# Seven half-size products for one more pair of row blocks, with the diagonal sums of two stages interleaved

## The chip, the cores and the metric

The kernel runs on one core of a Trainium2 chip. The metric is device time in microseconds (us) of one launch. Engines are named as in the profile: PE (TensorE matmuls), PEld (its weight loads), DVE (VectorE), ACT (ScalarE), POOL (GpSimd, which here also issues all large input loads) and SP (SyncE, which issues the output stores and the DMA transposes). The five engines run their own instruction streams in order and wait for one another through semaphores.

## The reference

A linear attention with decay (4 batches, 8 heads, 768 steps, head size 48) feeds a two-layer network with a leaky ReLU (384 to 2048 to 384, 3072 rows).

```python
# attention, for every batch and head
for t in range(768):
    cur = outer(u * k[t], v[t])
    y[t] = r[t] @ (state + cur)
    state = w[:, None] * state + outer(k[t], v[t])
# y is put side by side over the heads: x is 3072 x 384
h = x @ w_in                    # 384 x 2048
g = maximum(0.01 * h, h)
out = g @ w_out                 # 2048 x 384
```

## The kernel before

The 3072 rows are 24 **stages** of 128 steps (6 per batch) and 12 **pairs** of stages; pair m holds stages 2m and 2m+1. All compute is in bf16 with sums in fp32 in PSUM, which has eight banks, handed out in rotation by `next_bank`.

Work of a stage n, with the letter of its step:

- `prep` (P), DVE: r and k times powers of the decay, into `qk`; from stage 8 on, SP then turns it with a DMA transpose into `tp` (earlier stages use PE and ACT).
- `a_mm` (A), PE: the 128 x 128 scores of the eight heads, into two banks.
- `a_mask` (M), DVE: the scores are masked into `at`. From stage 8 on (`DIAG`), one predicated copy (line 408) writes the masked part over a tile that already holds the diagonal.
- `prep2` (Q): for stages below 8 it makes `vs`. From stage 8 on it makes the diagonal: three DVE operations, `ku = k*u` (line 346), `rku = r*ku` (348), and `s_tok`, the sum of `rku` over each head (350). Each needs the one before it, and a semaphore stands between them. Then `diag_tile` lays the eight sums on the diagonals of `at`: for stages 8 to 13 (below `LED`) POOL does it in two instructions (line 360), from 14 on ACT does it in eight (line 366).
- `kv_mm` (K), PE, and `state` (S), DVE: the new state from one bank and the old state (line 482, or lines 485 and 487).
- `y_part` (Y), PE and then ACT: the attention output, into `xT`.

Work of a pair: `g1_pair`, eight groups of six matmuls with `w_in` (line 562), each emptied by ACT with the leaky ReLU into `gT` (568); then the product with `w_out`, in one of two ways. `g2` (line 579) makes a stage's rows with 16 matmuls of 384 columns. `g2_seven` (line 643) makes a pair's four half-size blocks (128 rows x 192 columns each, 1024 of the 2048 inner terms at a time) out of seven products of 8 matmuls of 192 columns, in place of eight such products; for it DVE makes four sums of `gT` per pair (`g_sum`, line 617) and adds partial results from copies that ACT made (`keep`, line 651; `plus`, line 674). Its right-hand factors are four sums of `w_out`, made once by DVE (`w_sum`, line 599, four instructions). Before, pairs 4 to 11 use it (`SEVEN`).

The first stages are ordered by hand in `ORDER`, up to stage 9's masks. Then a loop over m from 3 to 11 emits, for one iteration: the eight `g1_pair` of pair m; the diagonal sums of stages 2m+4 and 2m+5 if they are below 14; the four `g_sum` of pair m-1 if it uses seven products; the diagonal sums of stages 2m+6 and 2m+7 if they are 14 or later; the loads of stages 2m+8 and 2m+9 (POOL, paced by the first group of pair m); scores and masks of stages 2m+4 and 2m+5; `y_part` of stages 2m+2 and 2m+3; `kv_mm` and `state` of 2m+4 and 2m+5; `prep` of 2m+6 and 2m+7; and last the product of pair m-1 with `w_out` (`second`). So pair 3's product is in the iteration of m = 4, between pairs 4 and 5 of `g1_pair`.

With seven products, one of the two `prep` and one of the two `state` are emitted inside `g2_seven`, and the 16 ACT tiles of stages 2m+6 and 2m+7 stand between its `keep` copies. `g2_seven` takes three banks: the two from which `y_part` was emptied, and the one from which the first `state` of the iteration reads. Its fourth product, `product(2, ...)`, writes that third bank:

```python
            product(1, 0, 0, True, False)
            keep(1, 1)
            some(3, 4)
            product(0, 1, 1, False, False)
            keep(0, 2)
            some(4, 16)
            product(2, (0, 1), (low, one), True, True)
            plus(2, 0, 0, 0)
```

Of the kernel before, what the change touches and what calls it, by code (L numbers as in the profile page):

```python
# [5 lines left out]
ALU = mybir.AluOpType  # L6
AF = mybir.ActivationFunctionType
AX = mybir.AxisListType
# [17 lines left out]
ORDER = """  # L26
P0 C F1 T0 P1 F1 T1.0 A0 T1.1 X0 M0 K0 W F1 V A1 Q0 X1 S0 Y0 M1 G0.0 K1 P2 T2 Q1 P3 Y1 T3 S1 X2 A2 M2 K2 G1.0 X3 A3 U J0.2 S2 Q2 M3 Y2 K3 P4
T4 Q3 J0.3 S3 Y3 J0.4 J0.5 J1.0 P5 A4 J1.1 P6 X4 M4 T5 X5 J1.2 K4 Q4 A5 S4 T6 J1.3 K5 J1.4 Y4 M5 L8 Q5 Y5 P7 J1.5 A6 J0.6 J2.0 J2.1 T7 M6 X6
X7 K6 J2.2 J2.3 A7 S6 J2.4 J2.5 L9 Q6 J0.7 J1.6 J2.6 M7 Z0 Z1 Z2 L10 J2.7 L11 J1.7 K7 S7 P8 Q7 Q8 P9 H0 Q9 K8 H1 P10 L12 K9 H2 S8 S9 Y6 Y7
A8 A9 P11 M8 H3 M9 L13  # L30
"""

# [5 lines left out]
class Sched:  # L38
# [8 lines left out]
    def add(self, eng, emit, R=(), W=(), dma=None):  # L47
        o = Op()
        o.eng, o.emit, o.dma, o.inc, o.val = eng, emit, dma, False, None
        deps = []  # L50
        for key in R:
            w = self.writer.get(key)
            if w is not None:
                deps.append((w, True))
        for key in W:
            w = self.writer.get(key)
            if w is not None:
                deps.append((w, False))
            for r in self.readers.get(key, ()):
                deps.append((r, False))  # L60
        o.deps = []
        for d, raw in deps:
            if d.dma is None and d.eng == eng and dma is None and (eng == "pe" or not raw):
                continue
            if d is not o and d not in o.deps:
                o.deps.append(d)
        for key in R:
            self.readers.setdefault(key, []).append(o)
        for key in W:
            self.writer[key] = o  # L70
            self.readers[key] = []
        self.ops.append(o)
        return o
# [47 lines left out]
def bass_rwkv5_eagle__then__act_leaky_relu_kernel(  # L121
# [13 lines left out]
    def SB(name, shape, dt=BF16):  # L135
        return ctx.enter_context(nc.sbuf_tensor(name, shape, dt))
# [1 line left out]
    NQK, NTP, NVS, NAT, NT, NX, NG, NO, NRK = 6, 6, 6, 6, 6, 3, 3, 4, 14  # L138
    TURNED, DIAG = 8, 8
    LED = 14  # L140
    SEVEN = (4, 5, 6, 7, 8, 9, 10, 11)
    HF, NH = NFB // 2, HD // 2
    w_in_sb = SB("w_in_sb", [128, NSL, DFF])
    w_out_sb = SB("w_out_sb", [128, NFB, HD])
# [24 lines left out]
    ident = SB("ident", [128, 128])  # L169
    ku = [SB(f"ku{i}", [128, HD]) for i in range(2)]  # L170
    rku = [SB(f"rku{i}", [128, HD]) for i in range(2)]
    s_tok = [SB(f"s_tok{i}", [128, H], FP32) for i in range(2)]
    qk = [SB(f"qk{i}", [128, 2 * H, E]) for i in range(NQK)]
    tp = [SB(f"tp{i}", [128, 2 * NP, 128]) for i in range(NTP)]
    vs = [SB(f"vs{i}", [128, HD]) for i in range(NVS)]
# [14 lines left out]
    add = sch.add  # L190
# [117 lines left out]
    def k_of(n):  # L308
        return k_sb[:, n % NRK, :] if n else k0_f[:, :]
# [26 lines left out]
    def prep2(n, whole=True):  # L336
        i2, iv = n % 2, n % NVS
        if n < DIAG:
            ps_s, key = kv_bank[n]
            s_of = ps_s[:, HD:HD + H]  # L340
            add("dve", lambda: V.tensor_tensor(hd(vs[iv][:, :]),  # L341
                                               v_sb[:, n, :].rearrange("p (h e) -> p h e", e=E)[:, :, 0:D],
                                               s_of.unsqueeze(2).to_broadcast([128, H, D]), ALU.mult),
                R=[("v", n), key], W=[("vs", iv)])
        else:
            add("dve", lambda: V.tensor_tensor(ku[i2][:, :], k_of(n), u_tab[:, :], ALU.mult),
                R=[("k", n % NRK), "u_tab"], W=[("ku", i2)])
            add("dve", lambda: V.tensor_tensor(rku[i2][:, :], r_of(n), ku[i2][:, :], ALU.mult),
                R=[("r", n % NRK), ("ku", i2)], W=[("rku", i2)])
            add("dve", lambda: V.tensor_reduce(s_tok[i2][:, :], hd(rku[i2][:, :]), AX.X, ALU.add),  # L350
                R=[("rku", i2)], W=[("s", i2)])
            if whole:
                diag_tile(n)

    def diag_tile(n, heads=range(H)):
        ia = n % NAT
        if n < LED:
            for hh in range(2):
                s_of = s_tok[n % 2][:, :].rearrange("p (m two) -> p two m", two=2)[:, hh, :]
                add("pool", lambda hh=hh, s_of=s_of: G.tensor_tensor(  # L360
                    at[ia][:, hh, :, :], ident[:, :].unsqueeze(1).to_broadcast([128, NP, 128]),
                    s_of.unsqueeze(2).to_broadcast([128, NP, 128]), ALU.mult),
                    R=["ident", ("s", n % 2)], W=[("at", ia, hh)])
            return
        for h in heads:
            add("act", lambda h=h: A.activation(at[ia][:, h % 2, h // 2, :], ident[:, :], AF.Copy,  # L366
                                                scale=s_tok[n % 2][:, h:h + 1]),
                R=["ident", ("s", n % 2)], W=[("at", ia, h % 2)])

    def turn(n, *halves):  # L370
        it, iq = n % NTP, n % NQK
# [363 lines left out]
    def u_table():  # L735
# [5 lines left out]
    steps = {"U": u_table, "V": u_cast, "P": prep, "Q": prep2, "T": turn, "A": a_mm, "M": a_mask, "K": kv_mm, "S": state, "Y": y_part, "X": diag, "C": decay_columns, "W": decay_table, "F": fill, "Z": w_sum,  # L741
             "G": g1, "J": g1_pair, "H": g2, "L": lambda n: load_stage(n, pace=[("pace", (n - 4) // 2, (n - 4) % 2)])}
    for name in ORDER.split():
        steps[name[0]](*(int(x) for x in name[1:].split(".") if x))
# [9 lines left out]
    for m in range(FIRST // 2, NST // 2):  # L754
        ahead = [n for n in (2 * m + 4, 2 * m + 5) if n < NST]
        further = [n for n in (2 * m + 6, 2 * m + 7) if LED <= n < NST]
        for j in range(8):
            g1_pair(m, j)
        for n in ahead:
            if n < LED:  # L760
                prep2(n)
        if m - 1 in SEVEN:
            for i in (0, 1, 3, 2):
                g_sum(m - 1, i)
        for n in further:
            prep2(n, False)
        for n in (2 * m + 8, 2 * m + 9):
            if n < NST:
                load_stage(n, pace=[("pace", 2 * m, 0)])
        for n in ahead:  # L770
            if n < DIAG:
                diag(n)
        for n in ahead:
            a_mm(n)
        for n in ahead:
            a_mask(n)
        y_first = taken[0] % 8
# [82 lines left out]
```

## Time and profile before

| | us |
|---|---|
| Median of 3 runs | 169.47 (167.68 to 171.02) |
| The profiled execution | 166.89 |
| Its span, first to last instruction | 165.0 |
| DVE busy in the span | 123.9 (75%) |
| ACT busy in the span | 116.3 (70%) |
| POOL busy in the span | 81.7 (50%) |

Times below are microseconds from the start of the span. In a row of the timeline stand start, busy time, engine, line and operation, and in brackets the engine's idle time before it and what ended it. In a row of the chain stand start, time, engine and line. An instruction's busy time can reach a little into the next one's, so the distance from start to start is what counts for an engine that has no pause.

### The profile page before, as it was taken

Reading aid. Unit: us, or ns where it says so; the run is one execution under the profiler, and the core shown is the slowest. Engines: PE = TensorE matmul, PEld = TensorE weight load, DVE = VectorE, ACT = ScalarE, POOL = GpSimd, SP = SyncE. Lnnn points to the kernel's source line nnn. Section 1 sums busy time; section 2 is a strip of 40 time slices with the busy share of each in tenths; the row PEclk is TensorE's granted clock in tenths of the full one; section 3 lists DMA queues with packets and bytes.
Section 4 is the critical chain, followed back from the end, with each engine's and each line's share of the span. In section 5 each row is a group of like instructions: output and inputs, shape, how many; then the busy total and the mean of one; then the engine's idle time right before and its main releaser. Section 6 shows DMA issues by size and latency. Waiting matters only on the chain.

```text
span 165.0 us, 5389 instructions
## 1 busy us (share of the span) xinstructions
PE 158.9 (96%) x2290; PEld 132.9 (81%) x2291; DVE 123.9 (75%) x238; ACT 116.3 (70%) x267; POOL 81.7 (50%) x97
## 2 busy tenths in 40 slices
PE   6979899999999999999999999999999999999993
PEld 3858678788666876876889889899899899898993
DVE  7797938657999979999668998878999467045253
ACT  4767588789113861989889989989999836828530
POOL 7999999992279989992750930920000000000000
PEclk9999999999999999999999999999999999999999
DMA  5999999999999999999995994996308102002022
GB/s 95 133 150 156 171 149 172 198 193 143 147 171 203 121 89 118 136 169 140 187 127 73 176 131 92 190 92 119 107 4 177 49 0 99 0 7 93 0 99 95
DMA packets 99260, 19.68 MB, mean 119 GB/s; under 512 B 92323, under 2 KB 99237, under 8 KB 99237
## 3 DMA queue, kind: packets, MB, share of 16 engines
q0 software_dynamic: 76512, 10.03, 96.9%
q1 hardware_dynamic: 21682, 9.11, 27.1%
q8 instruction: 18, 0.29, 0.8%
q10 hardware_dynamic: 1042, 0.20, 0.6%
q14 instruction: 6, 0.04, 0.1%
HBM read 20.45 MB, written 4.72 MB: 152 GB/s over the span
## 4 chain that ended last, share of the span: by engine, by line
PE 93%; DVE 4%; ACT 2%; issue 1%
PE ps_all L562 37%; PE ps_all L643 23%; PE ps_all L579 13%; PE ps_all L517 7%; PE ps_all L398 5%; PE ps_all L378 2%; PE ps_all L432 2%; DVE at L416 2%; PE ps_all L255 1%; ACT tp L385 1%; PE ps_all L295 1%; PE ps_all L456 1%; DVE vs L341 1%; PE ps_all L545 1%; ACT gT L568 0%
## 5 line engine op out<-in xcount | busy, mean ns | idle before, releaser
L562 PE MATMUL ps_all<-xT,w_in_sb 128*128 128x256 bf16 x564 | 64.8, 273 | 0.0
L562 PEld LDWEIGHTS ps_all<-xT,w_in_sb 128*128 128x128 bf16 x564 | 54.4, 98 | 7.1 <-DMA w_in_sb<-in_moe_w_in_dram 0.2
L568 ACT ACTIVATE gT<-ps_all 128x512 bf16<-128x512 f32 x94 | 54.7, 596 | 6.6 <-PE ps_all L562 3.0
L218 POOL DMA_DIRECT2D rk_sb<-in_k_dram x23 | 21.7, 942 | 17.0 <-PE ps_all L562 17.0
L366 ACT ACTIVATE at<-ident,s_tok 128x128 bf16<-128x128 bf16 x80 | 25.0, 390 | 0.0
L408 DVE CAST_PREDICATED at<-mask,ps_all 128x1024 bf16<-128x1024 uint16 x16 | 18.8, 1219 | 6.6 <-PE ps_all L398 6.5
L218 POOL DMA_DIRECT2D v_sb<-in_v_dram x24 | 22.7, 953 | 0.8 <-POOLq L845 0.8
L579 PE MATMUL ps_all<-w_out_sb,gT 128*128 128x384 bf16 x128 | 21.8, 326 | 0.0
L218 POOL DMA_DIRECT2D rk_sb<-in_r_dram x23 | 21.6, 943 | 0.0
L674 DVE TENSOR_TENSOR out_sb<-ps_all,snap 128x192 f32<-128x192 f32 x25 | 8.8, 356 | 14.9 <-PE ps_all L643 14.3
L579 PEld LDWEIGHTS ps_all<-w_out_sb,gT 128*128 128x128 bf16 x128 | 12.2, 98 | 7.7
L643 PE MATMUL ps_all<-tw,gs 128*128 128x192 bf16 x192 | 18.3, 246 | 0.0
L360 POOL TENSOR_TENSOR at<-ident,s_tok 128x512 bf16<-128x512 bf16 x12 | 13.4, 1142 | 8.2 <-DVE s_tok L350 8.2
L643 PEld LDWEIGHTS ps_all<-tw,gs 128*128 128x128 bf16 x192 | 16.1, 98 | 0.0
L585 ACT ACTIVATE out_sb<-ps_all 128x384 f32<-128x384 f32 x8 | 3.9, 488 | 14.6 <-PE ps_all L579 14.6
L532 ACT ACTIVATE xT<-ps_all 128x384 bf16<-128x384 f32 x24 | 11.0, 490 | 4.4 <-PE ps_all L517 4.1
L643 PE MATMUL ps_all<-w_out_sb,gT 128*128 128x192 bf16 x128 | 13.2, 246 | 0.0
L617 DVE TENSOR_TENSOR gs<-gT 128x1024 bf16<-128x1024 bf16 x16 | 10.9, 684 | 2.9 <-ACT gT L568 2.9
L517 PE MATMUL ps_all<-at,v_sb 128*32 128x128 bf16 x384 | 11.9, 224 | 0.3 <-DVE vs L341 0.2
L416 DVE TENSOR_TENSOR at<-ps_all,mask 128x512 bf16<-128x512 f32 x16 | 10.3, 682 | 2.1 <-PE ps_all L398 2.1
L651 ACT ACTIVATE snap<-ps_all 128x192 f32<-128x192 f32 x24 | 7.9, 330 | 4.8 <-PE ps_all L643 4.4
L517 PEld LDWEIGHTS ps_all<-at,v_sb 128*32 128x32 bf16 x384 | 9.1, 98 | 2.7 <-DVE vs L341 0.9
(80 smaller groups left out, 224.8 us busy)
## 6 DMA issues: line engine op xcount, KB each, us to landing
out_dram<-out_sb SPq DMA_DIRECT2D x22, 192.0 KB, 3.1
v_sb<-in_v_dram POOLq DMA_DIRECT2D x24, 96.0 KB, 5.5
rk_sb<-in_r_dram POOLq DMA_DIRECT2D x23, 96.0 KB, 5.8
rk_sb<-in_k_dram POOLq DMA_DIRECT2D x23, 96.0 KB, 5.6
w_in_sb<-in_moe_w_in_dram POOLq DMA_DIRECT2D x4, 384.0 KB, 6.6
w_out_sb<-in_moe_w_out_dram POOLq DMA_DIRECT2D x4, 384.0 KB, 10.3
out_dram<-out_sb SPq DMA_DIRECT2D x4, 96.0 KB, 1.6
tp<-qk SPq DMA_TRANSPOSE x16, 3.6
```

Source lines behind the costliest of these rows:

```text
L218: add("pool", lambda: G.dma_start(dst, src), R=pace, W=[key], dma=f"{which}{n}")
L360: add("pool", lambda hh=hh, s_of=s_of: G.tensor_tensor(at[ia][:, hh, :, :], ident[:, :].unsqueeze(1).to_broadcast([128, NP, 128]), s_of.un ...
L366: add("act", lambda h=h: A.activation(at[ia][:, h % 2, h // 2, :], ident[:, :], AF.Copy, scale=s_tok[n % 2][:, h:h + 1]), R=["ident", ("s" ...
L408: add("dve", lambda: V.copy_predicated(at[n % NAT][:, :, :, :].rearrange("p two m i -> p (two m) i"), mask[:, :].bitcast(mybir.dt.uint16). ...
L416: add("dve", lambda hh=hh, part=part: V.tensor_tensor(at[n % NAT][:, hh, :, :], part, mask[:, :].unsqueeze(1).to_broadcast([128, NP, 128]) ...
L517: last = PE.matmul(ps_y[32 * q:32 * q + 32, 128 * s:128 * s + 128], a, m, start=first_mm, stop=last_mm)
L532: add("act", lambda: A.activation(xT[m % NX][:, :, 128 * half:128 * half + 128], ps_y[:, 0:HD].rearrange("p (s t) -> p s t", t=128), AF.Copy),
L562: last = PE.matmul(ps_g[:, 256 * f:256 * f + 256], w_in_sb[:, s, 128 * fb:128 * fb + 128], xT[ix][:, s, :], start=s == 0, stop=s == NSL - 1)
L568: add("act", lambda: A.activation(gT[ig][:, 2 * j:2 * j + 2, :].rearrange("p f t -> p (f t)"), ps_g[:, :], AF.Prelu, alpha=0.01), R=[key], ...
L579: last = PE.matmul(ps_o[:, 0:HD], gT[ig][:, s, 128 * half:128 * half + 128], w_out_sb[:, s, :], start=s == 0, stop=s == NFB - 1)
L617: add("dve", lambda: V.tensor_tensor(x[i][:, :, :], a, b, op), R=keys, W=[("gs", m % 2, i)])
L643: done = PE.matmul(ps_o[:, 0:NH], lhs[:, s, :], rhs[:, s, :], start=first and s == 0, stop=s == HF - 1, skip_group_check=not (first and last))
```

## The change

Pair 3 joins the pairs with seven products. The three DVE operations of the diagonal sums are split into steps (`bonus`) and emitted for the two stages of a pair in alternation (`bonus_pair`), with the diagonal tiles of both stages behind them; `s_tok` gets four buffers in place of two. In `ORDER`, stage 9's `prep` goes ahead of the diagonal sums of stages 8 and 9, which are now together ahead of stage 4's product with `w_out`. The fourth `w_sum`, which ran behind the masks, states and `prep` of the iteration of m = 3, goes ahead of the masks of stages 10 and 11 in that iteration.

```diff
@@ ORDER
-X7 K6 J2.2 J2.3 A7 S6 J2.4 J2.5 L9 Q6 J0.7 J1.6 J2.6 M7 Z0 Z1 Z2 L10 J2.7 L11 J1.7 K7 S7 P8 Q7 Q8 P9 H0 Q9 K8 H1 P10 L12 K9 H2 S8 S9 Y6 Y7
+X7 K6 J2.2 J2.3 A7 S6 J2.4 J2.5 L9 Q6 J0.7 J1.6 J2.6 M7 Z0 Z1 Z2 L10 J2.7 L11 J1.7 K7 S7 P8 Q7 P9 B8 H0 K8 H1 P10 L12 K9 H2 S8 S9 Y6 Y7
...
-    SEVEN = (4, 5, 6, 7, 8, 9, 10, 11)
+    SEVEN = (3, 4, 5, 6, 7, 8, 9, 10, 11)
...
-    s_tok = [SB(f"s_tok{i}", [128, H], FP32) for i in range(2)]
+    s_tok = [SB(f"s_tok{i}", [128, H], FP32) for i in range(4)]
...
         else:
+            for step in range(3):
+                bonus(n, step)
+            if whole:
+                diag_tile(n)
+
+    def bonus(n, step):
+        i2, i4 = n % 2, n % 4
+        if step == 0:
             add("dve", lambda: V.tensor_tensor(ku[i2][:, :], k_of(n), u_tab[:, :], ALU.mult),
                 R=[("k", n % NRK), "u_tab"], W=[("ku", i2)])
+        elif step == 1:
             add("dve", lambda: V.tensor_tensor(rku[i2][:, :], r_of(n), ku[i2][:, :], ALU.mult),
                 R=[("r", n % NRK), ("ku", i2)], W=[("rku", i2)])
-            add("dve", lambda: V.tensor_reduce(s_tok[i2][:, :], hd(rku[i2][:, :]), AX.X, ALU.add),
-                R=[("rku", i2)], W=[("s", i2)])
-            if whole:
-                diag_tile(n)
+        else:
+            add("dve", lambda: V.tensor_reduce(s_tok[i4][:, :], hd(rku[i2][:, :]), AX.X, ALU.add),
+                R=[("rku", i2)], W=[("s", i4)])
+
+    def bonus_pair(n, whole=True):
+        for step in range(3):
+            bonus(n, step)
+            bonus(n + 1, step)
+        if whole:
+            diag_tile(n)
+            diag_tile(n + 1)
...
-        for n in ahead:
-            if n < LED:
-                prep2(n)
+        if ahead and ahead[0] < LED:
+            bonus_pair(ahead[0])
+        if m == 3:
+            w_sum(3)
         if m - 1 in SEVEN:
             for i in (0, 1, 3, 2):
                 g_sum(m - 1, i)
-        for n in further:
-            prep2(n, False)
+        if further:
+            bonus_pair(further[0], False)
...
         for n in coming[:at_once]:
             prep(n)
-        if m == 3:
-            w_sum(3)
```

More of the change, by code (lines that the diff above doesn't have):

```diff
@@ L358, in diag_tile @@
             for hh in range(2):
-                s_of = s_tok[n % 2][:, :].rearrange("p (m two) -> p two m", two=2)[:, hh, :]
+                s_of = s_tok[n % 4][:, :].rearrange("p (m two) -> p two m", two=2)[:, hh, :]
                 add("pool", lambda hh=hh, s_of=s_of: G.tensor_tensor(
@@ L362, in diag_tile @@
                     s_of.unsqueeze(2).to_broadcast([128, NP, 128]), ALU.mult),
[L363 removed]
+                    R=["ident", ("s", n % 4)], W=[("at", ia, hh)])
             return
@@ L366, in diag_tile @@
             add("act", lambda h=h: A.activation(at[ia][:, h % 2, h // 2, :], ident[:, :], AF.Copy,
-                                                scale=s_tok[n % 2][:, h:h + 1]),
-                R=["ident", ("s", n % 2)], W=[("at", ia, h % 2)])
+                                                scale=s_tok[n % 4][:, h:h + 1]),
+                R=["ident", ("s", n % 4)], W=[("at", ia, h % 2)])
     def turn(n, *halves):
@@ L739, in u_table @@
         add("act", lambda: A.activation(u_tab[:, :], ps_u[:, 0:HD], AF.Copy), R=[key], W=["u_tab"])
-    steps = {"U": u_table, "V": u_cast, "P": prep, "Q": prep2, "T": turn, "A": a_mm, "M": a_mask, "K": kv_mm, "S": state, "Y": y_part, "X": diag, "C": decay_columns, "W": decay_table, "F": fill, "Z": w_sum,
+    steps = {"U": u_table, "V": u_cast, "P": prep, "Q": prep2, "B": bonus_pair, "T": turn, "A": a_mm, "M": a_mask, "K": kv_mm, "S": state, "Y": y_part, "X": diag, "C": decay_columns, "W": decay_table, "F": fill, "Z": w_sum,
              "G": g1, "J": g1_pair, "H": g2, "L": lambda n: load_stage(n, pace=[("pace", (n - 4) // 2, (n - 4) % 2)])}
```

## The prediction

> **What bounds the kernel now.** I read the page's shares first, then the chain that ended last, then the chain in order of time, and then the timelines of DVE and POOL around the places that change.
>
> ```profile
> span 165.0 us, 5389 instructions
> PE 158.9 (96%) x2290; PEld 132.9 (81%) x2291; DVE 123.9 (75%) x238; ACT 116.3 (70%) x267; POOL 81.7 (50%) x97
> PEclk9999999999999999999999999999999999999999
> PE 93%; DVE 4%; ACT 2%; issue 1%
> ```
>
> PE is busy 96% of the span at full granted clock, and it is 93% of the chain. The chain in order of time says where the other 7% lies:
>
> ```profile
> 26.84 0.40 PE ps_all L398 x8
> ...
> 50.38 0.55 PE ps_all L398 x16
> ...
> 65.91 5.24 PE ps_all L562 x48
> 71.15 0.73 PE ps_all L398 x16
> ...
> 73.22 5.20 PE ps_all L579 x32
> 78.42 5.24 PE ps_all L562 x48
> ...
> 85.39 4.69 PE ps_all L643 x56
> 90.08 5.24 PE ps_all L562 x48
> ...
> 97.04 4.79 PE ps_all L643 x56
> ...
> 153.22 9.32 PE ps_all L643 x112
> ```
>
> From 26.84 to 162.54 the chain is PE alone, each piece starting where the last one ended. No other engine delays PE there. So nothing that DVE, ACT or POOL saves can shorten the run; only less PE work can, and the change can lose only where it makes PE wait for the first time. The question is therefore what PE saves in pair 3, and whether the extra DVE work around it stays ahead of PE.
>
> **What PE saves.** Pair 3's product is the row at 73.22: 32 matmuls, 5.20 us. Pair 4's by seven products is the row at 85.39: 56 matmuls, 4.69 us; pair 5's took 4.79. Pair 3 in that form is worth 5.20 - 4.69 = 0.51 us (0.41 by the other row). I take 0.51. That is all that the change can gain, 0.3% of the profiled execution.
>
> **What DVE saves and gets.** Three operations in a chain against three in alternation:
>
> ```profile
> 78.24 0.68 DVE L617 TENSOR_TENSOR gs<-gT 128x1024 bf16<-128x1024 bf16 x1
> 78.84 0.35 DVE L346 TENSOR_TENSOR ku<-rk_sb,u_tab 128x384 bf16<-128x384 bf16 x1
> 79.22 0.36 DVE L348 TENSOR_TENSOR rku<-rk_sb,ku 128x384 bf16<-128x384 bf16 x1
> 79.69 0.55 DVE L350 TENSOR_REDUCE s_tok<-rku 128x8 f32<-128x384 bf16 x1
> 80.16 0.35 DVE L346 TENSOR_TENSOR ku<-rk_sb,u_tab 128x384 bf16<-128x384 bf16 x1
> ...
> 86.89 0.36 DVE L487 TENSOR_TENSOR st<-sum_t,wl 128x384 bf16<-128x384 bf16 x1
> 87.16 0.55 DVE L319 TENSOR_TENSOR qk<-rk_sb,tab 128x768 bf16<-128x768 bf16 x1
> ```
>
> A stage takes 80.16 - 78.84 = 1.32, a pair 2.64. An operation of the same size followed by one that doesn't need it takes 0.27 from start to start (86.89 to 87.16), a reduction 0.47 (79.69 to 80.16). In alternation a pair is then 4 x 0.27 + 2 x 0.47 = 2.02, so 0.62 less. A rule of the Trainium skill speaks against this: VectorE: DVE Perf Modes, section "The DRAIN you can't avoid", has an operation wait for the pipe to empty whether or not a semaphore stands between. By it a pair would stay at 2.64 (the page excepts some operations with no wait between them). The trace doesn't agree: 0.38 behind a dependence (78.84 to 79.22) against 0.27.
>
> ```profile
> 76.18 0.68 DVE L617 TENSOR_TENSOR gs<-gT 128x1024 bf16<-128x1024 bf16 x1
> ```
>
> Against this stand four `g_sum`. Four of them took 2.66 (76.18 to 78.84, where the next operation starts), and the last, which nothing behind it depends on, 0.60 from start to start (78.24 to 78.84).
>
> **The hand-written part, stages 8 and 9.** No PE instruction moves. On DVE, stage 9's `prep` and its transpose come earlier, stage 8's sums later.
>
> ```profile
> 44.71 1.20 DVE L346 TENSOR_TENSOR ku<-rk_sb,u_tab 128x384 bf16<-128x384 bf16 x1
> ...
> 50.82 2.35 DVE L408 CAST_PREDICATED at<-mask,ps_all 128x1024 bf16<-128x1024 uint16 x2
> ```
>
> Stage 9's sums ran into POOL's diagonal of stage 8 (1.20 us for an operation that takes 0.35 elsewhere); together ahead of POOL they don't, while `prep` and two state updates now do. The masks of 8 and 9 start at 50.82 right behind the scores of stage 8 (PE from 50.38), so an earlier DVE gains nothing, and their output is needed one iteration later. I cost this at nothing; if the cover were gone, DVE would begin the next part some 0.85 us late, which the pause below takes up.
>
> **The moved sum of w_out.** In the iteration of m = 3 DVE looks like this:
>
> ```profile
> 53.09 0.35 DVE L346 TENSOR_TENSOR ku<-rk_sb,u_tab 128x384 bf16<-128x384 bf16 x1
> ...
> 54.73 2.94 DVE L348 TENSOR_TENSOR rku<-rk_sb,ku 128x384 bf16<-128x384 bf16 x1
> ...
> 59.32 2.35 DVE L408 CAST_PREDICATED at<-mask,ps_all 128x1024 bf16<-128x1024 uint16 x2 [1.07 <-PE ps_all L398]
> ...
> 63.39 0.95 DVE L599 TENSOR_TENSOR tw<-w_out_sb,tw 128x1536 bf16<-128x1536 bf16 x1
> 64.26 0.35 DVE L346 TENSOR_TENSOR ku<-rk_sb,u_tab 128x384 bf16<-128x384 bf16 x1
> ```
>
> The sums of stages 10 and 11 now end at 53.09 + 2.02 = 55.11, ahead of POOL's diagonals, and the 0.95 fits before the masks that wait for PE until 59.32. Moved there it costs nothing, and stage 12's sums start at 63.39 in place of 64.26. If POOL blocks it (below), the masks start late by up to 1.0, and the 0.87 saved behind them pays that back.
>
> **The iteration of m = 4 is the test.** POOL's diagonals and DVE's operations with two inputs in SBUF get in each other's way:
>
> ```profile
> 55.33 2.11 POOL L360 TENSOR_TENSOR at<-ident,s_tok 128x512 bf16<-128x512 bf16 x2
> 58.33 2.04 POOL L360 TENSOR_TENSOR at<-ident,s_tok 128x512 bf16<-128x512 bf16 x2 [0.89 <-DVE s_tok L350]
> ...
> 65.67 4.43 POOL L360 TENSOR_TENSOR at<-ident,s_tok 128x512 bf16<-128x512 bf16 x4
> ```
> ```profile
> 65.89 1.08 DVE L348 TENSOR_TENSOR rku<-rk_sb,ku 128x384 bf16<-128x384 bf16 x1
> 67.00 0.55 DVE L350 TENSOR_REDUCE s_tok<-rku 128x8 f32<-128x384 bf16 x1
> 67.47 0.61 DVE L346 TENSOR_TENSOR ku<-rk_sb,u_tab 128x384 bf16<-128x384 bf16 x1
> 68.12 1.08 DVE L348 TENSOR_TENSOR rku<-rk_sb,ku 128x384 bf16<-128x384 bf16 x1
> ...
> 71.52 2.35 DVE L408 CAST_PREDICATED at<-mask,ps_all 128x1024 bf16<-128x1024 uint16 x2 [0.16 <-PE ps_all L398]
> 73.79 0.55 DVE L482 TENSOR_TENSOR st<-ps_all,wl 128x384 bf16<-128x384 f32 x1
> ```
>
> POOL alone takes 1.02 an instruction (2.04 for two); the four at 65.67 take 4.43, and the DVE operations among them end where a POOL instruction ends (1.08 in place of 0.36), one for each, while the reduction keeps its 0.55. Four DVE operations cost POOL 4.43 - 4.08 = 0.35, or 0.09 each out of their 0.27.
>
> After the change: the sums of 12 and 13 run from 63.39 to 65.41, the first reduction ending near 64.95. POOL, with both earlier diagonals back to back and six loads behind them, is free by then, and runs its four instructions from 64.95. The four `g_sum` arrive at 65.41 behind the first of them. Taking turns, the last ends at 64.95 + 4.08 + 4e, where e is what one `g_sum` keeps POOL out: at least 0.60 - (0.27 - 0.09) = 0.42, at most 0.60. That is 70.71 to 71.43. The sums of 14 and 15, 2.02, are then free of POOL, which goes on to loads: 72.73 to 73.45. Then come the masks (2.27 from start to start, 71.52 to 73.79) and the state of stage 12 (0.55).
>
> What PE needs: the seven products start at 73.22, one in 4.69 / 7 = 0.67, and the fourth writes the bank that this state reads. It starts at 73.22 + 3 x 0.67 = 75.23, so the masks must start by 75.23 - 0.55 - 2.27 = 72.41. They start 0.32 to 1.04 late; PE waits that long. I take the middle, 0.68, since nothing in the trace shows which end is nearer: PE saves 0.51 and waits 0.68, a net +0.2.
>
> The Trainium skill, SBUF — State Buffer, section "SBUF: two separate sides", says that of a GpSimd operation and a VectorE one with two SBUF inputs the first holds the shared ports for its whole instruction and the other blocks fully. By it e is the upper 0.60 and the net +0.5. The trace agrees as to who blocks (1.08 against 0.36) but not that nothing overlaps, since POOL lost only 0.09 each.
>
> The rest hides. The ACT tiles of stages 14 and 15 need sums that are ready at about the end of `xT`, and the copies between them follow as in pair 4. The second `prep` and `state` move into the product; what they feed is needed one iteration later. A backlog on DVE ends in the next iteration, where it waited 2.48 for PE:
>
> ```profile
> 84.03 2.35 DVE L408 CAST_PREDICATED at<-mask,ps_all 128x1024 bf16<-128x1024 uint16 x2 [2.48 <-PE ps_all L398]
> ```
>
> Later iterations gain 0.62 of DVE time that PE doesn't wait for.
>
> **The rivals.** First, no collision that counts: POOL is late or DVE slips through, the masks start by 72.41, and the whole 0.51 is kept. For it: the `g_sum` and POOL start within half a microsecond of each other, and free of POOL the sums of 14 and 15 would end at 65.41 + 2.66 + 2.02 = 70.1. Against it: all four POOL instructions stand in that stretch. Time: -0.5.
>
> Second, slower: POOL passes DVE over. The 2.94 us row at 54.73 ended at 57.67, behind both POOL instructions of 55.33, so one operation can be passed over more than once. If that befalls `w_sum` as well (it ends only at about 60.3, its masks 1.0 late, stage 12's sums at 64.4) and then the `g_sum`, the first of these ends behind POOL's fourth instruction, near 66.0 + 4.4 = 70.4; with 2.05 more for the other three and 2.02 for the sums the masks start at 74.5 to 75.0, PE waits 2.1 to 2.6, and the net is +1.6 to +2.1. It turns against the kernel once the masks start later than 72.41 + 0.51 = 72.92; a loss of 2% (3.4 us) would need them at 76.3. For it is that one row; against it are the three rows from 65.89 to 68.12, in which the turn came after one POOL instruction.
>
> Third, alternation saves nothing: each operation still starts 0.38 to 0.47 behind the one before (78.84 to 80.16), the sums of 14 and 15 take 2.64, the masks start 0.62 later than in the likeliest case, and the net is +0.8. For it: no row shows two of these operations side by side; against it the 0.27 at 86.89. The rule of the skill named above would have it so.
>
> Fourth, the seven products of pair 3 may not take 4.69, because of its copies on ACT behind the tiles: 0.3 to 0.5 more. Pairs 4 and 5 with the same tiles argue against it.
>
> **How the numbers follow.** The likeliest case, taking turns, has 0.45; no collision 0.25; passed over 0.18; no saving by alternation 0.07; slow products and the rest 0.05. The profiled execution took 166.89, so the forecast is 167.1 there. The timed runs lie higher (median 169.47), and the change is the same microseconds: 169.47 + 0.2 = 169.7. Low end: 169.47 - 0.5 gives 169.0, less the distance from the median to the lowest run, 1.8, so 167.2. High end: +2.1 gives 171.6, and I put 171.8. Two per cent, 3.4 us, is about what a measurement of this kernel tells from no change. No case reaches it in either direction; the spread of the runs leaves 0.04 for faster, and that spread with the tail of the second rival 0.09 for slower.
>
> **What would show it.** The chain should have 56 matmuls of line 643 in pair 3, 4.7 us plus a wait for the state at line 482. The masks of stages 12 and 13 should start at 72.7 to 73.5, and a `g_sum` beside POOL should last about 1.4. `w_sum` should end before 59.3, and a pair of sums free of POOL should take 2.0. Masks at 71.5 mean the first rival; a chain with waits of PE elsewhere, or a difference over 2 us, would make the reasoning wrong.

## The result: slower by half a per cent

| | before | changed |
|---|---|---|
| Median, us (22 runs each) | 167.2 (166.45 to 171.6) | 168.16 (166.67 to 171.68) |
| Ratio to before, 95% interval | | 1.0054 [1.0033, 1.0074] |
| The profiled execution, us | 166.89 | 166.67 |
| Its span, us | 165.0 | 164.9 |

The changed kernel loses 0.9 us (0.0054 x 167.2), more than four times the 0.2 of the forecast. The three runs shown before the change had a median of 169.47; some executions of either kernel are disturbed, mostly in the first third, and the ratios leave these out. The profiled execution of the changed kernel is the fastest of its 22, so the two spans don't show the loss.

The page of the changed kernel, its first lines and the shares of its chain (lines of the code have moved by 16: 562 is now 578, 643 is 659, 482 is 498, 617 is 633, 408 is 424, 599 is 615, 360 is 376, 651 is 667; the three of the diagonal sums by 8 to 10: 346/348/350 are 354/357/360):

```profile
span 164.9 us, 5444 instructions
PE 158.7 (96%) x2315; PEld 134.0 (81%) x2315; DVE 123.7 (75%) x245; ACT 116.6 (71%) x269; POOL 83.1 (50%) x97
PE 91%; DVE 5%; ACT 1%; issue 1%; DVEq 0%
```

DVE now has 5% of the chain (4% before). The chain in order of time (start, time, engine and line) says where:

```profile
53.28 5.24 PE ps_all L578 x48
...
65.55 5.24 PE ps_all L578 x48
70.79 0.55 PE ps_all L414 x16
...
72.14 0.54 DVE s_tok L360
72.67 2.26 DVE at L424 x2
74.93 0.48 DVE st L498
...
75.45 2.88 PE ps_all L659 x32
78.33 5.24 PE ps_all L578 x48
84.13 0.73 PE ps_all L533 x44
85.30 4.69 PE ps_all L659 x56
...
153.13 9.32 PE ps_all L659 x112
```

From 27 us on PE waits for another engine only in pair 3's product: the last sum of stages 14 and 15, the masks of 12 and 13 and the state of 12 stand ahead of the last 32 of the 56 matmuls. The view of the waits names the same place (waiter, what ended the wait, total, times, longest):

```profile
PE ps_all L659 <- DVE st L498: 0.8, 1, 0.8
```

DVE and POOL in that iteration, from the timelines:

```profile
54.72 1.57 DVE L615 TENSOR_TENSOR tw<-w_out_sb,tw 128x1536 bf16<-128x1536 bf16 x1
...
63.03 0.62 DVE L354 TENSOR_TENSOR ku<-rk_sb,u_tab 128x384 bf16<-128x384 bf16 x2
...
65.02 1.30 DVE L633 TENSOR_TENSOR gs<-gT 128x1024 bf16<-128x1024 bf16 x1
66.36 1.42 DVE L633 TENSOR_TENSOR gs<-gs,gT 128x1024 bf16<-128x1024 bf16 x1
67.81 1.42 DVE L633 TENSOR_TENSOR gs<-gT,gs 128x1024 bf16<-128x1024 bf16 x1
69.15 1.53 DVE L633 TENSOR_TENSOR gs<-gT 128x1024 bf16<-128x1024 bf16 x1
70.60 0.61 DVE L354 TENSOR_TENSOR ku<-rk_sb,u_tab 128x384 bf16<-128x384 bf16 x2
...
72.59 2.34 DVE L424 CAST_PREDICATED at<-mask,ps_all 128x1024 bf16<-128x1024 uint16 x2
```
```profile
54.44 4.76 POOL L376 TENSOR_TENSOR at<-ident,s_tok 128x512 bf16<-128x512 bf16 x4
...
64.73 5.39 POOL L376 TENSOR_TENSOR at<-ident,s_tok 128x512 bf16<-128x512 bf16 x4 [0.26 <-DVE s_tok L360]
```

This is the likeliest case of the prediction, row by row: the four `g_sum` take turns with POOL's four instructions, and the masks start 72.59 - 53.28 = 19.31 behind the start of pair 3's `g1_pair`, where the forecast had 72.73 to 73.45 less 53.64, that is 19.1 to 19.8.

From here on one figure is compared between profiles, the **stretch** from the start of pair 3's `g1_pair` to the start of the last product (both rows of the chain); what happens ahead of it differs from execution to execution of one kernel. Before it is 153.22 - 53.64 = 99.58, in the profile above 153.13 - 53.28 = 99.85: 0.27 more, near the 0.2 of the forecast. So the question that the experiments had to answer: where do the timed executions lose the other 0.6?

### The profile page after: what moved, and what is told of

Read it like the earlier page. It is cut to its first block, busy times and chain, and to the rows that moved or that the text cites. A ratio compares the mean times of both kernels' runs of the same rounds, so it can differ in the third digit from the quotient of the medians.

```text
span 164.9 us, 5444 instructions
## 1 busy us (share of the span) xinstructions
PE 158.7 (96%) x2315; PEld 134.0 (81%) x2315; DVE 123.7 (75%) x245; ACT 116.6 (71%) x269; POOL 83.1 (50%) x97
## 4 chain that ended last, share of the span: by engine, by line
PE 91%; DVE 5%; ACT 1%; issue 1%; DVEq 0%
PE ps_all L578 37%; PE ps_all L659 25%; PE ps_all L595 10%; PE ps_all L533 7%; PE ps_all L414 4%; PE ps_all L394 3%; PE ps_all L448 2%; DVE at L432 2%; PE ps_all L255 1%; DVE at L424 1%; PE ps_all L295 1%; PE ps_all L472 1%; ACT tp L401 1%; DVE st L498 1%; PE ps_all L561 1%
## 5 line engine op out<-in xcount | busy, mean ns | idle before, releaser
L690 DVE TENSOR_TENSOR out_sb<-ps_all,snap 128x192 f32<-128x192 f32 x28 | 9.9, 356 | 16.1 <-PE ps_all L659 15.1
L659 PE MATMUL ps_all<-tw,gs 128*128 128x192 bf16 x216 | 20.6, 246 | 0.0
L376 POOL TENSOR_TENSOR at<-ident,s_tok 128x512 bf16<-128x512 bf16 x12 | 14.7, 1256 | 6.8 <-DVE s_tok L360 6.7
L659 PEld LDWEIGHTS ps_all<-tw,gs 128*128 128x128 bf16 x216 | 18.1, 98 | 0.0
L595 PE MATMUL ps_all<-w_out_sb,gT 128*128 128x384 bf16 x96 | 16.4, 326 | 0.0
L633 DVE TENSOR_TENSOR gs<-gT 128x1024 bf16<-128x1024 bf16 x18 | 13.8, 765 | 2.9 <-ACT gT L584 2.9
L659 PE MATMUL ps_all<-w_out_sb,gT 128*128 128x192 bf16 x144 | 14.9, 246 | 0.8 <-DVE st L498 0.8
L595 PEld LDWEIGHTS ps_all<-w_out_sb,gT 128*128 128x128 bf16 x96 | 9.1, 98 | 5.8
L601 ACT ACTIVATE out_sb<-ps_all 128x384 f32<-128x384 f32 x6 | 2.9, 491 | 14.4 <-PE ps_all L595 14.4
L659 PEld LDWEIGHTS ps_all<-w_out_sb,gT 128*128 128x128 bf16 x144 | 11.8, 98 | 1.3 <-DVE st L498 1.0
L667 ACT ACTIVATE snap<-ps_all 128x192 f32<-128x192 f32 x27 | 8.9, 330 | 4.9 <-PE ps_all L659 4.4
```

The lines of the kernel that those rows point to most:

```text
L376: add("pool", lambda hh=hh, s_of=s_of: G.tensor_tensor(at[ia][:, hh, :, :], ident[:, :].unsqueeze(1).to_broadcast([128, NP, 128]), s_of.un ...
L595: last = PE.matmul(ps_o[:, 0:HD], gT[ig][:, s, 128 * half:128 * half + 128], w_out_sb[:, s, :], start=s == 0, stop=s == NFB - 1)
L633: add("dve", lambda: V.tensor_tensor(x[i][:, :, :], a, b, op), R=keys, W=[("gs", m % 2, i)])
L659: done = PE.matmul(ps_o[:, 0:NH], lhs[:, s, :], rhs[:, s, :], start=first and s == 0, stop=s == HF - 1, skip_group_check=not (first and last))
```

## The experiments

**The changed kernel again, unedited.** Four more comparisons on other chips, the last beside e14 and e15.

> The changed kernel once more, unedited, for a second profile: its first one took 166.67 us while the median of its runs is 168.16. Port theory (POOL's diagonals of stages 12 and 13 hold up the four g_sum, and the fourth of the seven products waits for the state of stage 12): an execution of about 168.1 shows the only PE wait after 27 us there, but some 2 us long in place of 0.8. Start theory (the extra time lies in the hand-ordered part before 50 us, where loads arrive): the wait in pair 3's product stays 0.8 and the iteration of m = 3 begins about 1.4 us later than the 53.3 of the first profile.

> The changed kernel a third time, beside the two above. Port theory: 1.004 to 1.008 again, and in its profile a wait of 0.8 to 2 us in pair 3's product alone. Start theory: an execution near the median shows the iteration of m = 3 beginning later than 54.0.

> The changed kernel beside the two above on the same chip: 1.004 to 1.010 by either theory; a profile of an execution in which a g_sum is passed over by the whole burst, if one falls so, shows a wait of about 1.5 to 2 us in pair 3's product by the arrival theory.

> The changed kernel unedited, on the same chip as the two others, as their measure: 1.004 to 1.009 over the kernel before.

Ratios 1.0065 [1.0029, 1.0101], 1.0096 [1.0065, 1.0127], 1.0073 [1.0043, 1.0104] and 1.0051 [1.0006, 1.0095]. The loss is real, and 0.3 us would be a ratio of only 1.0016. The profiles of the first three show the wait of 0.8 and stretches of 99.85 to 99.87. The fourth shows something else. The ends of its stretch, its DVE and its POOL:

```profile
53.60 5.24 PE ps_all L578 x48
...
154.45 9.32 PE ps_all L659 x112
```

```profile
55.05 5.30 DVE L615 TENSOR_TENSOR tw<-w_out_sb,tw 128x1536 bf16<-128x1536 bf16 x1
60.28 2.34 DVE L424 CAST_PREDICATED at<-mask,ps_all 128x1024 bf16<-128x1024 uint16 x2
...
64.33 0.62 DVE L354 TENSOR_TENSOR ku<-rk_sb,u_tab 128x384 bf16<-128x384 bf16 x2
...
73.90 2.34 DVE L424 CAST_PREDICATED at<-mask,ps_all 128x1024 bf16<-128x1024 uint16 x2
```
```profile
54.55 0.93 POOL L218 DMA_DIRECT2D v_sb<-in_v_dram  x1
55.44 4.09 POOL L376 TENSOR_TENSOR at<-ident,s_tok 128x512 bf16<-128x512 bf16 x4
```

And its waits of PE in pair 3's product:

```profile
PE ps_all L659 <- DVE st L498: 1.4, 1, 1.4
PE ps_all L659 <- ACT snap L667: 0.2, 1, 0.2
```

`w_sum` started 0.39 ahead of POOL's burst of four diagonals, to which POOL came straight from a load, and ended behind all four: 5.30 us for an operation that takes 0.95 alone, while POOL ran at its undisturbed pace (4.09 for four). The masks of 10 and 11 start late, the sums of 12 at 64.33 instead of 63.03, and from there on everything is as in the first profile, `g_sum` by turns included. The masks of 12 and 13 are 20.30 behind the start of `g1_pair` (73.90 - 53.60), 0.99 later than in the profile above, PE waits 1.6, and the stretch is 154.45 - 53.60 = 100.85, 1.27 over the kernel before. In the first profile `w_sum` began 0.28 behind POOL's first instruction, in the middle of it, and took its turn after 1.57. So the same kernel has two outcomes, 0.27 and 1.27, and the two profiles differ by 0.67 us in when `w_sum` starts against POOL. The execution with the passing-over took 167.98, the median of its 12 runs is 168.22; the first profile's 166.67 and the second's 167.40 were the fastest of their 22 and 10.

**Parts of the change alone.** First without pair 3 among the seven products, then only that (with the fourth `w_sum` ahead of the masks, as in the change), then with the old hand-written order.

```diff
e2  -    SEVEN = (3, 4, 5, 6, 7, 8, 9, 10, 11)
e2  +    SEVEN = (4, 5, 6, 7, 8, 9, 10, 11)
```


> The alternation, the new order and the earlier sum of w_out stay; pair 3 goes back to 32 matmuls of 384 columns and the four g_sum leave that iteration. Port theory: no wait of PE in the iteration of m = 4, ratio to the kernel before 0.998 to 1.001. Start theory: the loss stays, ratio 1.004 to 1.007.

1.0000 [0.9974, 1.0027]; no wait of PE in the iteration of m = 4, stretch 99.41. The alternation, the new order and the moved `w_sum` are together worth nothing that the timed runs can tell (0.27% is 0.45 us); the stretch is 0.17 shorter.

```diff
e3  (the kernel before, with)
-    SEVEN = (4, 5, 6, 7, 8, 9, 10, 11)
+    SEVEN = (3, 4, 5, 6, 7, 8, 9, 10, 11)
...
+        if m == 3:
+            w_sum(3)
         if m - 1 in SEVEN:
...
-        if m == 3:
-            w_sum(3)
```


> Only pair 3 by seven products, with the sum of w_out ahead of the masks of stages 10 and 11; no alternation, old order. Port theory: the chain of DVE in m = 4 is up to 1.2 us longer than in the changed kernel, the masks of stages 12 and 13 start 0.6 to 1.2 us later and PE waits that much longer: ratio 1.007 to 1.012. Start theory: the loss goes with the new order, ratio 0.997 to 1.002.

1.0285 [1.0224, 1.0346]. The timelines of DVE and PE:

```profile
56.07 2.56 DVE L348 TENSOR_TENSOR rku<-rk_sb,ku 128x384 bf16<-128x384 bf16 x1
...
66.58 2.97 DVE L348 TENSOR_TENSOR rku<-rk_sb,ku 128x384 bf16<-128x384 bf16 x1
...
76.78 2.34 DVE L408 CAST_PREDICATED at<-mask,ps_all 128x1024 bf16<-128x1024 uint16 x2
```
```profile
76.55 0.83 PE L643 MATMUL ps_all<-tw,gs 128*128 128x192 bf16 x8 [0.77 <-ACT snap L651]
79.65 1.46 PE L643 MATMUL ps_all<-w_out_sb,gT 128*128 128x192 bf16 x8 [2.27 <-DVE st L482]
```

And the chain behind that wait:

```profile
79.65 4.33 PE ps_all L643 x32
```

Passed over twice, by two POOL instructions each time, and without alternation the sums of 14 and 15 are 0.6 longer: PE waits 3.0. The loss is more than this wait. Behind it the last 32 matmuls took 4.33 instead of the 2.88 of the changed kernel, and the profile shows a granted clock of 0.50 for PE from 79.65 to 82.18. With alternation and the same old order (e6, next) the loss is 0.95%, so alternation keeps the seven products of pair 3 from costing nearly 3%.

```diff
e6  -... P8 Q7 P9 B8 H0 K8 H1 P10 L12 ...
e6  +... P8 Q7 Q8 P9 H0 Q9 K8 H1 P10 L12 ...
```


> As the changed kernel, but stages 8 and 9 in the hand-written order of before (sums of 8, prep of 9, product of stage 4, sums of 9); alternation in the loop, the moved sum of w_out and seven products for pair 3 stay. Start theory: the loss was made in this order, ratio 0.999 to 1.003. Port theory: nothing changes, ratio 1.004 to 1.008, the wait of 0.8 in pair 3's product stays.

1.0095 [1.007, 1.0121]. Its profile shows the passing-over again, the `w_sum` this time 0.38 ahead of POOL (55.96), and waits of 1.4 and 0.4; its stretch is 101.05:

```profile
55.58 5.29 DVE L615 TENSOR_TENSOR tw<-w_out_sb,tw 128x1536 bf16<-128x1536 bf16 x1
```

With the old order the loss is that of the unedited kernel on the same chip (1.0096, e7), so the hand-written part is not the cause. (H0 in these lines is stage 0's product with `w_out`; the section on the change says stage 4's.)

**POOL out of the way, or the state earlier.** Three ways to remove the wait: the diagonals of 12 and 13 on ACT, the state of 12 between the two masks, and no diagonals of 12 and 13 at all.

```diff
e4  -    LED = 14
e4  +    LED = 12
```


> As the changed kernel, but LED = 12: the diagonals of stages 12 and 13 are made by ACT, 16 tiles in the iteration of m = 3 ahead of pair 2's product, and their sums by DVE in that iteration's pause; POOL has no diagonal left in m = 4. Port theory: the four g_sum take 0.7 each, no PE wait in pair 3's product, the 0.5 us of its seven products is kept: ratio 0.996 to 0.998. Start theory: ratio 1.002 to 1.005.

1.0013 [0.9973, 1.0052]. The four `g_sum` take 0.68 to 0.69, PE doesn't wait in pair 3, the stretch is 98.90, or 0.68 under before. The time doesn't follow all the way; in m = 3 the sums of stage 13 came before the load of its k (DVE waited 0.78), and `g1_pair` of pair 3 began at 54.86 in this profile.

```diff
e5, e15
-        for n in ahead:
+        split = m == 4
+        for n in ahead[:1] if split else ahead:
             a_mask(n)
...
         for n in turning[:at_once]:
             state(n)
+        if split:
+            a_mask(ahead[1])
```


> As the changed kernel, but in the iteration of m = 4 alone the state of stage 12 goes between the masks of stages 12 and 13, not behind both. The bank that the fourth of pair 3's products needs is then free 1.1 us earlier. Port theory, with the whole loss in that wait (0.8 us in the profiles, about 1.7 in the executions at the median): in the profile the wait of 0.8 is gone and pair 3's product takes 4.7; ratio to the kernel before 0.996 to 0.999, and 1.000 to 1.002 if the wait of the median execution is longer than the 1.1 won. Start theory: only the 0.8 goes, ratio 1.000 to 1.003.

> The changed kernel with the state of stage 12 between the masks of stages 12 and 13 in the iteration of m = 4, once more. If its 1.0006 was no accident: 0.998 to 1.003. If it was: 1.004 to 1.008, as for the changed kernel itself.

1.0006 [0.9976, 1.0037] beside 1.0096 for the unedited kernel on the same chip, and 0.999 [0.9951, 1.0029] beside 1.0051. One mask takes 1.13, and moving it behind the state gains 0.9% and 0.6%, that is 1.0 to 1.5 us. The wait of 0.8 costs the stretch 0.96 (99.85 against 98.89 in e14, where PE waits for nothing there), so no more than this could come back if the first profile were the usual case. That points to a longer wait in the usual execution, though the intervals still reach 0.96. The profile of e5 has a third form of the passing-over, with `g_sum` (0.28 ahead of POOL's 65.84) as its victim:

```profile
65.56 4.93 DVE L633 TENSOR_TENSOR gs<-gT 128x1024 bf16<-128x1024 bf16 x1
70.53 0.69 DVE L633 TENSOR_TENSOR gs<-gs,gT 128x1024 bf16<-128x1024 bf16 x1
71.25 0.69 DVE L633 TENSOR_TENSOR gs<-gT,gs 128x1024 bf16<-128x1024 bf16 x1
71.86 0.69 DVE L633 TENSOR_TENSOR gs<-gT 128x1024 bf16<-128x1024 bf16 x1
```

The other three then run free. The first mask starts at 74.46, and with the state right behind it PE waits 0.7 for a copy of ACT and 0.3 for the state.

```diff
e14      def diag_tile(n, heads=range(H)):
e14  +       if n in (12, 13):
e14  +           return
```


> The changed kernel in which POOL does not lay the sums of stages 12 and 13 on the diagonals of their tiles (the diagonals of these two stages are left out; everything else is issued as before). Nothing of POOL but loads is then left beside DVE in the iteration of m = 4. Theory that the whole loss comes from POOL and DVE sharing a way into SBUF there: the four g_sum take about 0.7 each, the masks of stages 12 and 13 start near 70, PE does not wait in pair 3's product, and the ratio to the kernel before is 0.995 to 0.998. Rival, that timed executions lose by something else that seven products in pair 3 bring (ACT's copies, banks, the shorter span between xT and the product): the same profile, and a ratio of 1.003 or more.

0.9944 [0.9906, 0.9982] beside 1.0051 for the unedited kernel on the same chip. The chain of pair 3's product and the timeline of its `g_sum` (lines two further down here):

```profile
75.98 4.68 PE ps_all L661 x56
```
```profile
68.32 0.68 DVE L635 TENSOR_TENSOR gs<-gT 128x1024 bf16<-128x1024 bf16 x1
69.04 0.69 DVE L635 TENSOR_TENSOR gs<-gs,gT 128x1024 bf16<-128x1024 bf16 x1
69.76 0.69 DVE L635 TENSOR_TENSOR gs<-gT,gs 128x1024 bf16<-128x1024 bf16 x1
70.37 0.68 DVE L635 TENSOR_TENSOR gs<-gT 128x1024 bf16<-128x1024 bf16 x1
...
74.46 2.36 DVE L426 CAST_PREDICATED at<-mask,ps_all 128x1024 bf16<-128x1024 uint16 x2 [0.74 <-PE ps_all L416]
```

With POOL's four instructions left out and nothing else changed in the code (POOL's next loads come earlier), the loss is a gain, and the stretch is 155.47 - 56.58 = 98.89, 0.69 under before: the saving of the seven products, and 0.17 that e2 shows too. So the loss needs these diagonals, and the profile shows how: without them the four `g_sum` take 0.68 to 0.69 each. Between this kernel and the unedited one lie 1.07%, or 1.8 us, nearer to 100.85 - 98.89 = 1.96 than to 99.85 - 98.89 = 0.96, but the intervals reach both. The run fits both outcomes: the masks now wait 0.74 for PE, and a `w_sum` passed over would cost them 1.0 out of that and of the 0.7 by which the state then still precedes the fourth product (75.98 + 3 x 0.67 = 77.99, against 74.46 + 2.27 + 0.55 = 77.28).

**Moving work to avoid the collision.** Three kernels have earlier loads (so that POOL is idle when the sums are ready), in e10 with the sums of 12 and 13 an iteration earlier too; two have the four `g_sum` ahead of the sums of 12 and 13. None came out as expected.

```diff
e8, e9, e10 (ORDER; e9 has the split of e5 too)
-... L10 J2.7 L11 J1.7 K7 S7 P8 Q7 P9 B8 H0 K8 H1 P10 L12 K9 H2 S8 S9 Y6 Y7
-A8 A9 P11 M8 H3 M9 L13
+... L10 J2.7 L11 L12 L13 J1.7 K7 S7 P8 Q7 P9 B8 H0 K8 H1 P10 K9 H2 S8 S9 Y6 Y7
+A8 A9 P11 M8 H3 M9
e10
-    LED = 14
+    LED = 12
...
+        if m == 3:
+            bonus_pair(further[0], False)
...
-        if further:
+        if further and m > 3:
```


> As the changed kernel, but POOL issues the loads of stages 12 and 13 right behind those of stage 11, in the time in which it waited for the sums of stage 8. Then no load stands between its diagonals of stages 8, 9 and 10, 11, and each burst of diagonals starts on a sum that DVE has just made, so that the DVE operation behind that sum always comes second. Arrival theory (a DVE operation with two SBUF inputs that is issued just ahead of a burst waits for the whole burst; one that comes after the burst's start gets a turn behind each instruction): w_sum and the g_sum never last over 1.7 us, the wait of 0.8 in pair 3's product stays, ratio to the kernel before 1.000 to 1.003. If the loss at the median has another cause: 1.004 to 1.008 as before.

> The early loads and the state of stage 12 between the masks of stages 12 and 13. Arrival theory: no starving and no wait of PE in pair 3's product, all of the 0.5 us is kept: ratio 0.995 to 0.998. If not: 0.999 to 1.003 as with the split alone.

> The early loads, and the diagonals of stages 12 and 13 on ACT (LED = 12), their sums by DVE ahead of those of stages 10 and 11, so that POOL's burst starts behind them. Arrival theory: w_sum takes turns with POOL (about 1.6 us), the four g_sum take 0.7 each, no wait of PE in the iterations of m = 3 and m = 4, ratio 0.995 to 0.998. If not: 1.000 to 1.004 as with LED = 12 alone.

1.0136 [1.0063, 1.0209], 1.0040 [0.999, 1.0089] and 1.0121 [1.0039, 1.0204]. In e8 POOL starts every burst on DVE's sum, as meant, and the stretch is 99.85 as by turns; its profiled execution is the longest of its six (173.72), so where the others lose 1.4% isn't shown. By the ratios the split gains some 1% here too, though the intervals overlap. e9 has no wait in pair 3, but PE waits 0.77 for a DMA transpose behind it (88.61). In e10 the sums came ahead of their loads: DVE waited 3.90 for one k and 2.72 for another.

```diff
e11, e12 (e12 has the split of e5 too)
+        if m == 4:
+            for i in (0, 1, 3, 2):
+                g_sum(m - 1, i)
         if ahead and ahead[0] < LED:
...
-        if m - 1 in SEVEN:
+        if m > 4 and m - 1 in SEVEN:
```


> As the changed kernel, but in the iteration of m = 4 the four g_sum go ahead of the sums of stages 12 and 13. Then POOL's burst for 12 and 13 starts on a sum that DVE makes behind them, POOL having waited for it, and no load ends just before it. The DVE operations that share time with the burst are the four of the sums of 14 and 15, one turn each. Arrival theory: the g_sum take 0.7 each, the masks of 12 and 13 start some 0.1 us later than in the turn-taking profiles of the changed kernel, the wait for the state of stage 12 is 0.8 to 0.9 in every execution, ratio to the kernel before 1.000 to 1.004. If the executions at the median lose their time elsewhere: 1.005 to 1.010, as the changed kernel.

> Both: the g_sum ahead of the sums of 12 and 13, and the state of stage 12 between the masks of 12 and 13. Arrival theory: no wait of PE in pair 3's product in any execution, the 0.5 us is kept, ratio 0.995 to 0.998. Otherwise 0.999 to 1.003, as with the split alone.

1.0152 [1.0106, 1.0199] and 1.0122 [1.0067, 1.0178]. The collision only changes its victims. The `g_sum` are free (0.68 each), and the sums of 14 and 15 take turns with POOL's burst at 68.24:

```profile
68.53 2.08 DVE L354 TENSOR_TENSOR ku<-rk_sb,u_tab 128x384 bf16<-128x384 bf16 x2
70.53 2.31 DVE L357 TENSOR_TENSOR rku<-rk_sb,ku 128x384 bf16<-128x384 bf16 x2
```

PE waited 1.0 for the state in that profile of e11, and in the one of e12 0.97 for a DMA transpose (87.25). e11's stretch is some 0.45 us (0.3%) longer than by turns, but its ratio is 0.8% above that of the unedited kernel on the same chip (1.0073, e13). Where the rest goes is open.

**`w_sum` out of POOL's way.** If the usual execution is the one with `w_sum` passed over, putting it ahead of the sums of 10 and 11, where POOL can't have started, should leave the 0.27.

```diff
e17, e18 (e18 has the split of e5 too)
+        if m == 3:
+            w_sum(3)
         if ahead and ahead[0] < LED:
             bonus_pair(ahead[0])
-        if m == 3:
-            w_sum(3)
```


> The changed kernel with the fourth w_sum ahead of the sums of stages 10 and 11 in the iteration of m = 3, so that it is done before POOL can start their diagonals and can't be passed over by them. Theory that the median execution of the changed kernel has w_sum passed over by all four POOL instructions (a wait of PE of 1.4 to 1.6 in pair 3's product, against 0.8 where w_sum takes its turn): w_sum takes 0.95, the masks of stages 10 and 11 follow the scores, the four g_sum still take turns with POOL, PE waits about 0.8 for the state of stage 12, ratio 0.999 to 1.003. Rival, that w_sum passed over is rare and something else in the sharing makes the median: 1.005 to 1.009 as for the changed kernel.

> The same with the state of stage 12 between the masks of stages 12 and 13 in the iteration of m = 4, which brings it forward by 1.13. Theory: the wait of 0.8 goes too, PE does not wait in pair 3's product, ratio 0.995 to 0.998. Rival: 0.999 to 1.003, as for the split alone, if the early w_sum gains nothing.

1.003 [0.9995, 1.0064] and 1.0002 [0.9957, 1.0047]. The mechanism came as meant, `w_sum` free of POOL and a wait of 0.8, and the stretch is 99.85:

```profile
55.49 0.95 DVE L615 TENSOR_TENSOR tw<-w_out_sb,tw 128x1536 bf16<-128x1536 bf16 x1
...
61.73 2.35 DVE L424 CAST_PREDICATED at<-mask,ps_all 128x1024 bf16<-128x1024 uint16 x2 [3.28 <-PE ps_all L414]
```

The ratio is below every one of the five for the unedited kernel (1.0051 to 1.0096), as the theory wants, but its interval reaches both theories' numbers, and the unedited kernel wasn't timed on that chip. e18 shows no wait in pair 3 and a stretch of 98.89; its interval holds the 0.996 that this would be, and 1 as well. No kernel here that computes everything was shown to beat the one before.

| kernel | `w_sum` lasts | PE waits in pair 3's product | stretch | ratio |
|---|---|---|---|---|
| before | 0.95 | none | 99.58 | 1 |
| changed, first profile | 1.57 | 0.8 | 99.85 | 1.0054 |
| changed, e16 | 5.30 | 1.6 | 100.85 | 1.0051 |
| e6, old order | 5.29 | 1.8 | 101.05 | 1.0095 |
| e17, `w_sum` first | 0.95 | 0.8 | 99.85 | 1.003 |
| e15, split | 1.56 | none | 98.91 | 0.999 |
| e14, no diagonals of 12, 13 | 1.56 | none | 98.89 | 0.9944 |

## Why the prediction was too small

**Right: what bounds the kernel, and what PE saves.** Undisturbed, pair 3's product took 4.68 (e14), as the 4.69 taken from pair 4. Nothing that DVE saved elsewhere shortened the timed runs (e2). One row of that chain was slower than it had to be, though: the scores at 71.15 took 0.73 before and 0.55 in the changed kernel (70.79), which is about the 0.17 by which e2's stretch is shorter. The fourth rival, slow products, is out where `g_sum` goes by turns; where DVE was later still, PE also waited for a copy of ACT (0.2 in e16, 0.4 in e6, 0.7 in e5, 0.8 in e3).

**Right: alternation.** A pair of sums free of POOL took 72.59 - 70.60 = 1.99, forecast 2.02; the third rival is out, and with it the reading of the Trainium skill (VectorE: DVE Perf Modes, "The DRAIN you can't avoid") by which it would have stayed at 2.64.

**Right: the hand-written part and the pause behind it.** It cost nothing that a run could tell (e2, e6).

**Right: the place, and turn-taking.** The burst of four starts at 64.73 and the last `g_sum` ends at 70.60 (the start behind it), so e is (70.60 - 64.73 - 4.08) / 4 = 0.45, near the lower end of 0.42 to 0.60 and not the upper one, which it would be by the Trainium skill (SBUF — State Buffer, "SBUF: two separate sides"). The wait was 0.79, forecast 0.32 to 1.04 with 0.68 in the middle; the net of that execution 0.27, forecast 0.2. That the net came so near is partly luck: the 0.17 of the scores was not in the sum, and neither was what the 32 matmuls behind the wait took in addition, 2.88 against 4/7 of 4.68 = 2.67. The two nearly cancel.

**The first rival, no collision,** needs POOL out of that place: e14 gives -0.69 in the stretch (0.17 of it the scores) and 0.9944 [0.9906, 0.9982], where it said -0.5 (a ratio of 0.997).

**Wrong: the price of the moved `w_sum`.** The prediction put it at nothing: "If POOL blocks it (below), the masks start late by up to 1.0, and the 0.87 saved behind them pays that back." But the sum for m = 4 had already spent this 0.87, by starting the sums of stage 12 at 63.39. Both can't hold. With `w_sum` passed over, the sums start 1.0 later, and so do the masks of 12 and 13: in e16 by 0.99, with PE's waits 1.6 and the stretch 1.27 over before. The passing-over was on the page of before, as the 2.94 us row, and the second rival had `w_sum` meet it, but only together with `g_sum`, at +1.6 to +2.1 and with a chance of 0.18. The case that came, `w_sum` passed over and `g_sum` by turns, at about 0.2 + 1.0 = +1.2, was not priced at all. What the timed runs say (0.9 to 1.6 us in five comparisons) is nearer to 1.27 than to 0.27.

The change itself makes this worse than the 2.94 us row of before showed. There POOL laid the diagonals of stages 10 and 11 two by two and waited for DVE's second sum in between, so that an operation could be passed over by two at most. With both stages' diagonals behind both sums, four stand back to back, and `w_sum` was put right where they begin.

**What is shown and what isn't.** Shown by e2 and e14: the loss needs the seven products of pair 3 and the diagonals of 12 and 13 together. Shown by profiles: the two outcomes and their size. Pointed to by the split on the same chips: a usual wait of more than 0.8. Not shown: that `w_sum` passed over is the usual outcome. One profile of five of the unedited kernel has it, two of the other four were the fastest of their runs, and e17 points that way without settling it; timed executions leave no trace. e5's passed-over `g_sum` may have its share too.

The times of the first comparison look like two outcomes as well. Of the 22 of the kernel before, 12 lie from 166.45 to 167.28, with a median of 166.80. Of the changed kernel's, four lie from 166.67 to 167.16 and ten from 167.84 to 168.47, with medians 0.24 and 1.32 above that. But a single time doesn't tell which outcome it had: e7's profiled execution took 168.15 by turns, with its `g1_pair` of pair 3 beginning late, at 54.77. Late starts alone don't explain the ten: e2, whose code is the same up to there, began at 54.77 in an execution of 167.72, yet eight of its 12 times lie from 166.73 to 167.15.

## What to carry to other kernels

When two moves draw on the same slack, write the slack down once and subtract both: here 0.87 us behind the masks was spent on an earlier start and counted again as cover for a late `w_sum`. A DVE operation with two SBUF inputs that lands just ahead of a burst of GpSimd instructions can cost the whole burst, so batching GpSimd work back to back raises the price of one bad arrival from two instructions to four. And where a profile comes from the fastest of many executions, compare a stretch of it and the median, and expect a second outcome behind a difference that the profile doesn't show.

## What the runs showed of the hardware

Of a DVE operation and POOL's burst, the one that starts first doesn't win. DVE operations that started 0.22 to 0.64 ahead of a burst were passed over by all of it (2.94 before, 2.56 and 2.97 in e3, 5.29, 5.30 and 4.93), while those that started during an instruction of POOL went in behind it (1.3 to 1.6). But in e5 a `w_sum` that started 0.65 ahead of POOL took only 1.56. Why one arrival is passed over and another not stays open. It is not what the Trainium skill (SBUF — State Buffer, "SBUF: two separate sides") has, by which the first holds the ports for its whole instruction.

A wait of PE can cost more than its length: in e3 a wait of 2.27 was followed by 2.5 us at a granted clock of 0.50, while behind the 1.4 of e16 the clock stayed at 1.00.

Unedited, the same kernel began pair 3's `g1_pair` at 53.28, 53.60, 54.00, 54.77 or 59.76. Some of that is twelve early matmuls that took 0.83 in one execution and 1.44 in another; the first row is of the changed kernel's first profile, the second of e7, with the clock granted in full in both:

```profile
11.69 0.83 PE ps_all L561 x12
```
```profile
12.06 1.44 PE ps_all L561 x12
```
